# Last chunk's columns in token order, two stores for each PSUM set, and the last evictions shared by two engines

## The chip, the cores and the metric

The kernel runs on one core of a Trainium2 chip. The metric is the device time of one execution in microseconds, and the number used is the median over several executions. PE is the matrix engine (TensorE), DVE is VectorE, ACT is ScalarE, POOL is GpSimd and SP is SyncE, which here issues most DMAs. PSUM is the memory that PE writes its sums to; SBUF is the working memory of the other engines.

## What is computed

Strided sparse attention on 8 batches, 8 heads, 576 positions and 64 columns a head, and after it a dense layer with a rational activation on the 4608 tokens:

```python
scores = scale * np.matmul(q, k.transpose(0, 1, 3, 2))
mask_local = (rel >= 0) & (rel < 32)                        # heads 0..3
mask_strided = (rel >= 0) & (pos[None, :] % 32 == pos[:, None] % 32)   # heads 4..7
attn = softmax(where(mask, scores, -1e9))
x = (attn @ v) as [4608, 512]                               # tokens by (head, column)
h = x @ w_in                                                # 512 -> 2048
P = a[0] + a[1] * h + a[2] * h**2 + a[3] * h**3
Q = 1.0 + abs(b[0]) * abs(h) + abs(b[1]) * h**2
out = (P / (Q + 1e-6)) @ w_out                              # 2048 -> 512, float32
```

## The kernel before

**Chunks.** The dense layer works on nine chunks of 512 tokens. Chunks 0 to 7 are the first 512 positions of each batch. Chunk 8 (NCH - 1) holds the last 64 positions of all eight batches; its inputs are gathered in XW by one transpose for each batch, while chunks 0 to 7 take theirs from XT.

**One chunk.** `dense1(c)` multiplies by w_in: for each pair of the 16 blocks of hidden columns PE fills one PSUM set of two banks (128 x 2 x 512), and ACT copies it to HB as bf16 (L972, the "eviction"). In every chunk the columns of HB are tokens in a permuted order: in chunk 8 the order is (batch, g, i), where position 512 + 4 i + g of the batch is meant. DVE then works out numerator and denominator with nine kinds of instruction (L986 to L1037), and ACT takes 1/Q as Exp of minus Ln (L1010, L1013). L1037 multiplies the two and ends the activation. `dense2(c)` multiplies by w_out: two PSUM sets for each chunk, i2 = 0 and 1, each with two blocks of 128 tokens. A set is evicted to one of two f32 buffers OS (L1103 on ACT, and for the last set of chunk 8 L1100 on DVE) and goes out with four stores of 128 KB (L1060), one for each block (e_) and each half of the partitions (z). SP issues them.

**The last chunk.** Chunk 8 is also the tail of the kernel (`tail`). Its two sets lie in PSUM "A" and "S" (set A and set S here) and are filled in turn, in steps of two blocks of hidden columns, as L1037 delivers them. Its activation is done in groups of 8, 4, 2 and 2 blocks; of the other late chunks each is one group of 16.

**Attention.** One step of the main loop takes one batch: loads of q, k and v by POOL, scores on PE, Exp on ACT, the product with v on PE, normalisation on DVE (L878, L880) into XR, and a DMA transpose of XR into XT or XW (L910, issued by SP). The transposes of q and k into sT (L673) and of the rest of q and k into LT (L684) are SP's, too; a small copy from LT to kL is ACT's (L687), written with a step of 4 elements.

**The order of work.** Every operation is given to `add(engine, instruction, dependencies, cost, key, ...)`. The order in which each engine works is written out by hand in `ORDER`: the n-th operation added has rank ORDER[n], and each engine's queue is sorted by rank. Costs and keys do not enter. Where an operation depends on another engine's, a wait for a semaphore is put in front of it, and an engine's queue is never left out of order: what stands behind a waiting instruction waits, too. On SP this holds for stores and transposes in one queue.

Of the kernel before, what the change touches and what calls it, by code (L numbers as in the profile page):

```python
# [6 lines left out]
AF = mybir.ActivationFunctionType  # L7
# [8 lines left out]
def _bf16_bits(x):  # L16
# [7 lines left out]
    3, 10, 7, 85, 6, 136, 33, 29, 40, 17, 30, 32, 16, 78, 80, 31, 34, 88, 90, 69, 96, 43, 72, 60, 42, 39,  # L24
    74, 45, 103, 112, 64, 110, 105, 91, 101, 92, 62, 1, 14, 5, 21, 8, 28, 4, 24, 13, 12, 15, 11, 2, 9, 52,
    56, 61, 41, 59, 94, 133, 137, 20, 23, 27, 44, 49, 51, 19, 18, 25, 22, 55, 83, 87, 68, 53, 71, 66, 26,
    36, 47, 50, 35, 46, 57, 65, 54, 58, 75, 79, 82, 86, 115, 67, 70, 73, 98, 102, 95, 97, 100, 108, 111, 93,
    99, 106, 114, 117, 77, 107, 116, 129, 128, 132, 135, 139, 183, 37, 81, 76, 84, 104, 126, 130, 109, 122,
    123, 121, 120, 127, 113, 48, 38, 89, 63, 145, 147, 0, 118, 153, 163, 156, 166, 134, 143, 142, 146, 150,
    157, 154, 164, 170, 176, 119, 125, 138, 140, 148, 152, 167, 151, 155, 160, 169, 171, 175, 124, 131, 158,  # L30
    162, 165, 179, 188, 173, 178, 180, 185, 216, 223, 161, 172, 174, 186, 189, 192, 195, 211, 234, 200, 208,
    214, 218, 226, 263, 196, 206, 191, 198, 212, 221, 219, 229, 240, 248, 258, 285, 310, 264, 299, 267, 270,
    282, 290, 301, 318, 181, 184, 187, 190, 193, 182, 194, 204, 209, 224, 228, 231, 233, 244, 255, 236, 239,
    245, 249, 259, 177, 201, 205, 253, 250, 256, 266, 278, 283, 144, 141, 149, 159, 210, 215, 197, 217, 203,
    202, 213, 199, 207, 220, 168, 227, 235, 238, 274, 271, 243, 241, 222, 232, 284, 225, 297, 230, 237, 242,
    246, 252, 257, 260, 262, 265, 269, 261, 276, 279, 308, 320, 293, 298, 300, 302, 303, 306, 309, 313, 312,
    315, 317, 319, 321, 326, 327, 329, 335, 356, 381, 399, 268, 273, 272, 281, 287, 307, 311, 324, 333, 336,
    342, 350, 357, 367, 371, 296, 305, 288, 294, 328, 334, 338, 346, 383, 347, 363, 374, 382, 390, 403, 314,
    322, 304, 316, 331, 340, 325, 332, 353, 378, 385, 418, 441, 406, 427, 392, 398, 429, 447, 457, 459, 254,
    251, 247, 291, 289, 348, 349, 286, 280, 292, 344, 295, 277, 275, 339, 355, 351, 341, 395, 394, 366, 369,  # L40
    364, 361, 362, 358, 323, 330, 337, 343, 365, 370, 376, 380, 386, 393, 387, 405, 408, 417, 415, 411, 419,
    421, 425, 430, 434, 435, 437, 438, 445, 446, 449, 450, 454, 455, 458, 460, 485, 533, 540, 345, 354, 352,
    360, 359, 373, 368, 377, 379, 389, 384, 388, 396, 401, 391, 397, 409, 424, 436, 448, 487, 475, 511, 467,
    476, 500, 529, 568, 581, 453, 481, 488, 503, 512, 535, 557, 592, 400, 413, 422, 433, 439, 523, 532, 442,
    520, 443, 451, 456, 462, 471, 543, 536, 558, 547, 404, 375, 372, 431, 416, 428, 412, 410, 423, 426, 414,
    402, 420, 407, 474, 495, 466, 477, 517, 514, 486, 504, 505, 497, 489, 508, 490, 510, 499, 479, 472, 468,
    463, 465, 461, 452, 432, 440, 464, 469, 483, 491, 494, 498, 506, 470, 509, 515, 525, 526, 542, 546, 548,
    549, 550, 553, 555, 561, 563, 566, 567, 572, 571, 576, 579, 582, 583, 611, 636, 661, 473, 480, 484, 496,
    507, 521, 537, 544, 528, 539, 545, 551, 559, 564, 552, 560, 570, 580, 584, 664, 675, 593, 624, 600, 605,
    639, 685, 651, 700, 603, 612, 617, 637, 658, 674, 689, 719, 478, 493, 502, 518, 556, 671, 627, 693, 668,  # L50
    565, 575, 587, 595, 599, 744, 737, 647, 735, 482, 524, 444, 541, 501, 534, 522, 538, 530, 516, 492, 513,
    531, 519, 586, 597, 594, 596, 620, 623, 589, 616, 609, 606, 608, 590, 602, 610, 625, 622, 630, 604, 527,
    554, 578, 562, 573, 577, 585, 588, 598, 615, 621, 631, 569, 591, 640, 646, 648, 650, 655, 656, 659, 666,
    669, 672, 678, 676, 680, 681, 684, 683, 686, 688, 690, 694, 708, 726, 789, 601, 619, 626, 635, 642, 660,
    654, 662, 663, 670, 677, 682, 687, 692, 667, 679, 697, 704, 710, 756, 792, 769, 784, 728, 733, 803, 819,
    749, 813, 721, 746, 752, 771, 777, 791, 798, 832, 607, 613, 632, 698, 711, 804, 748, 801, 806, 715, 730,
    739, 759, 781, 886, 840, 884, 812, 574, 634, 645, 657, 653, 638, 629, 641, 618, 649, 614, 644, 633, 628,
    709, 699, 706, 702, 741, 731, 723, 718, 727, 720, 716, 701, 712, 724, 738, 732, 729, 773, 652, 643, 665,
    673, 691, 696, 703, 707, 713, 717, 722, 743, 695, 740, 750, 763, 762, 766, 770, 776, 780, 786, 790, 797,
    814, 800, 807, 815, 818, 817, 822, 823, 825, 827, 860, 874, 878, 705, 714, 725, 736, 753, 765, 767, 775,  # L60
    774, 779, 783, 787, 794, 799, 778, 795, 809, 816, 824, 871, 894, 879, 889, 843, 847, 858, 922, 911, 916,
    839, 855, 861, 876, 883, 892, 900, 934, 788, 805, 811, 821, 828, 837, 905, 882, 834, 833, 849, 865, 887,
    899, 910, 931, 936, 907, 764, 734, 772, 768, 757, 758, 745, 754, 760, 742, 755, 761, 747, 751, 848, 830,
    838, 836, 880, 872, 869, 859, 853, 864, 846, 857, 867, 862, 844, 850, 842, 852, 793, 782, 785, 796, 802,
    810, 820, 826, 829, 835, 841, 854, 808, 831, 863, 870, 866, 895, 897, 898, 901, 902, 908, 909, 914, 915,
    918, 919, 921, 923, 925, 926, 928, 929, 946, 961, 963, 845, 851, 856, 868, 873, 877, 875, 885, 881, 888,
    890, 893, 896, 903, 891, 906, 913, 920, 927, 957, 967, 943, 948, 940, 942, 954, 970, 973, 978, 935, 947,
    950, 956, 962, 971, 975, 981, 904, 912, 917, 924, 930, 937, 939, 933, 966, 932, 938, 952, 958, 964, 997,
    996, 990, 993, 941, 945, 949, 953, 955, 960, 944, 951, 965, 969, 972, 976, 979, 983, 959, 980, 984, 991,
    994, 1008, 1025, 1012, 1029, 1000, 1003, 1044, 1048, 1017, 1035, 1001, 1005, 1009, 1018, 1023, 1030,  # L70
    1040, 1053, 968, 974, 977, 982, 986, 1019, 992, 987, 998, 988, 995, 1004, 1007, 1011, 1015, 1013, 1034,
    1016, 985, 989, 999, 1006, 1010, 1021, 1002, 1024, 1038, 1047, 1049, 1064, 1072, 1060, 1078, 1059, 1063,
# [210 lines left out]
def bass_strided_sparse_attn__then__act_rational_pade_kernel(nc, q, k, v, moe_w_in, moe_w_out, moe_a, moe_b, out):  # L283
# [11 lines left out]
    P = 34.0  # L295
# [44 lines left out]
    OS = [A(f"OS{i}", [128, 2, 512], F32) for i in range(NO)]  # L340
# [277 lines left out]
    def ca(n):  # L618
        return 0.19 + n * 0.000833
# [554 lines left out]
```

## Time and profile before

| what | value |
|---|---|
| median of 11 runs | 370.87 us (367.21 to 376.05) |
| profiled execution, its own time | 370.07 us |
| profiled execution, its span | 368.3 us |
| instructions | 9765 |
| PE / DVE / ACT / POOL busy in the span | 86% / 85% / 77% / 41% |
| last matmul ends | 352.3 us |
| last eviction ends | 353.5 us |
| stores | 72 of 128 KB |

The profile is of one execution, with times from the start of its span. The span is 1.8 us shorter than the execution's own time, and that execution ran 0.8 us below the median. Busy shares are averages over stages that differ: up to about 86 us inputs and the first batches set the time, from there to 290 us attention and dense work are mixed, and from 290 us only the dense layer's last two to three chunks are left.

### The profile page before, as it was taken

To read this page: it belongs to the slowest core of one execution; us is meant where nothing else is said; L and a number is where in the kernel's file an instruction comes from. 1 tells how busy PE (TensorE), PEld (TensorE's weight loads), DVE (VectorE), ACT (ScalarE), POOL (GpSimd) and SP (SyncE) were. 2 spreads that over 40 slices of the span, in tenths; PEclk is the share of its full clock that TensorE was granted. 3 is DMA by queue.
4 is the path that set the end of the run, shared out by engine and by line. 5 is a ranking of instruction groups with operands and counts; after the bars stand their busy time and mean duration, and the time that the engine had idled before them with its cause. 6 is when DMAs were issued, how large, how long until landed. Compare 5 with 4: busy or idle time off the path is not lost.

```text
span 368.3 us, 9765 instructions
## 1 busy us (share of the span) xinstructions
PE 316.5 (86%) x4350; PEld 160.4 (44%) x4388; DVE 311.8 (85%) x280; ACT 285.1 (77%) x233; POOL 149.2 (41%) x216
## 2 busy tenths in 40 slices
PE   0669797998999999999699996999999999999920
PEld 0445455444455444544254453444444455554400
DVE  0464999979999997998799899967999899999910
ACT  1324988987998996899789999599899699978510
POOL 1899598308930894498069706600000000000000
PEclk9999999999999999999989999899999999999985
DMA  8999989999978899998989699814501212213212
GB/s 215 214 127 199 204 91 142 139 191 77 126 98 117 89 131 144 147 113 86 167 84 150 65 139 126 111 44 74 102 0 23 59 41 63 67 45 77 51 40 74
DMA packets 95481, 39.12 MB, mean 106 GB/s; under 512 B 66640, under 2 KB 90384, under 8 KB 95440
## 3 DMA queue, kind: packets, MB, share of 16 engines
q0 software_dynamic: 55104, 16.79, 46.4%
q1 hardware_dynamic: 40336, 21.72, 29.8%
q8 instruction: 34, 0.56, 0.7%
q14 instruction: 7, 0.06, 0.1%
HBM read 36.90 MB, written 9.44 MB: 126 GB/s over the span
## 4 chain that ended last, share of the span: by engine, by line
PE 60%; DVE 19%; DMA 10%; SPq 4%; issue 3%; ACT 1%; DVEq 0%
PE psO L613 28%; PE psH L613 18%; PE psS L613 9%; DMA XT<-XR 4%; PE psA L613 4%; DVE XR L880 2%; DVE T L1031 2%; DMA T<-in_v_dram 2%; DVE T L1037 2%; DVE UU L1001 2%; DMA XW<-XR 2%; DMA sT<-qn 2%; DVE T L1029 2%; DVE T L986 1%; DVE UU L998 1%
## 5 line engine op out<-in xcount | busy, mean ns | idle before, releaser
L613 PE MATMUL psO<-Wout,T 128*128 128x512 bf16 x478 | 110.9, 379 | 5.2 <-issue 2.9
L613 PE MATMUL psH<-XT,Win 128*128 128x512 bf16 x336 | 81.8, 385 | 4.0 <-DMA XT<-XR 3.9
L1010 ACT ACTIVATE UU<-UU,cst 128x2048 bf16<-128x2048 bf16 (+1 forms) x38 | 72.2, 1911 | 1.8 <-DVE UU L1001 1.8
L613 PEld LDWEIGHTS psO<-Wout,T 128*128 128x128 bf16 x512 | 48.4, 98 | 57.2 <-issue 1.4
L1013 ACT ACTIVATE UU<-UU 128x2048 bf16<-128x2048 bf16 (+1 forms) x38 | 68.9, 1823 | 0.1
L972 ACT ACTIVATE HB<-psH 128x1024 bf16<-128x1024 f32 x48 | 49.1, 1022 | 15.7 <-PE psH L613 14.7
L613 PEld LDWEIGHTS psH<-XT,Win 128*128 128x128 bf16 x336 | 30.7, 97 | 42.6 <-DMA XT<-XR 4.3
L1037 DVE TENSOR_TENSOR T<-T,UU 128x4096 bf16<-128x4096 bf16 (+2 forms) x23 | 41.9, 1821 | 1.6 <-ACT UU L1013 1.5
L1001 DVE TENSOR_TENSOR UU<-UU,T 128x4096 bf16<-128x4096 bf16 (+2 forms) x23 | 41.9, 1821 | 0.3
L1027 DVE TENSOR_TENSOR T<-T,HB 128x8192 bf16<-128x8192 bf16 (+3 forms) x17 | 41.0, 2414 | 0.2
L1031 DVE TENSOR_TENSOR T<-T,HB 128x8192 bf16<-128x8192 bf16 (+3 forms) x17 | 40.9, 2408 | 0.1
L505 POOL DMA_DIRECT2D VL<-in_v_dram x24 | 19.9, 834 | 47.9 <-PE psA L613 47.4
L998 DVE TENSOR_SCALAR UU<-T,coef 128x4096 bf16<-128x4096 bf16 (+2 forms) x23 | 26.2, 1139 | 0.3
L880 DVE TENSOR_TENSOR XR<-psA,RC 128x512 bf16<-128x512 f32 (+1 forms) x35 | 21.9, 624 | 4.2 <-DMA XT<-XR 1.8
L1020 ACT ACTIVATE T<-HB,coef 128x4096 bf16<-128x4096 bf16 x6 | 22.8, 3796 | 3.1 <-DVE UU L1001 3.1
L526 POOL DMA_DIRECT2D VT<-in_v_dram x32 | 24.4, 782 | 0.2 <-issue 0.2
L1029 DVE TENSOR_SCALAR T<-T,coef 128x8192 bf16<-128x8192 bf16 (+3 forms) x17 | 23.4, 1376 | 0.2
L484 POOL DMA_DIRECT2D tm<-in_q_dram x32 | 20.6, 648 | 6.8 <-DMA HB<-in_q_dram 6.8
L613 PE MATMUL psO<-XT,Win 128*128 128x512 bf16 x96 | 22.7, 378 | 0.7 <-ACT HB L972 0.7
L484 POOL DMA_DIRECT2D tm<-in_k_dram x32 | 21.3, 692 | 4.3 <-DMA LT<-tm 4.3
L1034 DVE TENSOR_SCALAR T<-T,coef 128x8192 bf16<-128x8192 bf16 (+3 forms) x17 | 22.8, 1342 | 0.2
L475 POOL DMA_DIRECT2D kn<-in_k_dram x14 | 15.1, 1082 | 19.1 <-PE psS L613 10.4
(166 smaller groups left out, 460.3 us busy)
## 6 DMA issues: line engine op xcount, KB each, us to landing
out_dram<-OS SPq DMA_DIRECT2D x72, 128.0 KB
kn<-in_k_dram POOLq DMA_DIRECT2D x14, 256.0 KB, 7.4
qn<-in_q_dram POOLq DMA_DIRECT2D x14, 256.0 KB, 7.4
Win<-in_moe_w_in_dram POOLq DMA_DIRECT2D x4, 512.0 KB, 8.3
Wout<-in_moe_w_out_dram POOLq DMA_DIRECT2D x1, 2048.0 KB, 18.9
VL<-in_v_dram POOLq DMA_DIRECT2D x24, 72.0 KB, 3.7
HB<-in_k_dram SPq DMA_DIRECT2D x2, 512.0 KB, 5.9
HB<-in_q_dram SPq DMA_DIRECT2D x2, 512.0 KB, 6.3
```

The source lines that it names most:

```text
L484: add("POOL", (lambda e, h=h, r0=r0: e.dma_start(tm[r0:r0 + 16, :].rearrange("x (g y d) -> x y g d", g=4, y=2)[:, h % 2], src[b, h, 512:57 ...
L613: return lambda e: e.matmul(out_ap, l, r, start=start, stop=stop, skip_group_check=True)
L880: o3 = add("DVE", (lambda d, rc=rc, x=x, src=src, nh_=nh_: d.tensor_tensor(x[:, 0:64 * nh_].rearrange("x (h d) -> x h d", h=nh_), src[:, : ...
L972: o2 = add("ACT", (lambda a, hb=hb, ps=ps, f=f: a.activation(hb[:, f:f + 2, :], ps[:, :, :], AF.Copy)), [o1, old], ca(1024), key.of("HB"))
L998: d2 = add("DVE", (lambda d, u=u, t3=t3, sl=sl, HG=HG: d.tensor_scalar(u[:, 0:HG, :], t3[:, sl, :], b1_ap, b0_ap, op0=Alu.mult, op1=Alu.add)),
L1001: d3 = add("DVE", (lambda d, u=u, t3=t3, sl=sl, HG=HG: d.tensor_tensor(u[:, 0:HG, :], u[:, 0:HG, :], t3[:, sl, :], op=Alu.mult)), [d2], ct ...
L1010: ln = add("ACT", (lambda a, u=u, zl=zl: a.activation(u[:, zl, :], u[:, zl, :], AF.Ln, bias=cst[:, 0:1], scale=1.0)), [d3, cons], 0.28 + w ...
L1013: ex.append(add("ACT", (lambda a, u=u, zl=zl: a.activation(u[:, zl, :], u[:, zl, :], AF.Exp, scale=-1.0)), [ln], 0.21 + w * 0.000833, kz + ...
L1027: d5 = add("DVE", (lambda d, hb=hb, t3=t3, g_=g_: d.tensor_tensor(t3[:, g_, :], t3[:, g_, :], hb[:, g_, :], op=Alu.mult)), [d4], ctt(n), k ...
L1029: d6 = add("DVE", (lambda d, t3=t3, g_=g_: d.tensor_scalar(t3[:, g_, :], t3[:, g_, :], a_ap[1], None, op0=Alu.add)), [d5], cts(n, 1), key ...
L1031: d7 = add("DVE", (lambda d, hb=hb, t3=t3, g_=g_: d.tensor_tensor(t3[:, g_, :], t3[:, g_, :], hb[:, g_, :], op=Alu.mult)), [d6], ctt(n), k ...
L1037: d9 = add("DVE", (lambda d, t3=t3, u=u, sl=sl, HG=HG: d.tensor_tensor(t3[:, sl, :], t3[:, sl, :], u[:, 0:HG, :], op=Alu.mult)), [d8, ex], ...
```

## The change

It has four parts.

1. In chunk 8, ACT's eviction L972 writes HB in token order (batch, i, g). It reads PSUM as before, in the order (batch, g, i), and so writes runs of 16 elements with a step of 4. The DVE work and the matmuls after it use HB's columns as they come, so the rows of set A and set S are in token order too.
2. A set goes out with two stores of 256 KB instead of four of 128 KB, one for each half of the partitions, with both blocks e in it. For chunks 0 to 7 the rows written are the same. For chunk 8 the destination of a store was 4 x 16 x 512 (g, i, column) and is 64 x 2 x 512 (row, e, column) now.
3. Each of the last two sets is evicted by two engines: ACT copies the first block (512 columns) and DVE the second. A store of these sets depends on both.
4. `ORDER` is a new list of 1113 ranks (before 1147: 36 stores fewer, 2 half evictions more), and it places operations on all engines anew.

Read against the order in which the program adds its operations, the new list does this, in outline. At the start, SP's loads of q, k and v for batch 0 are issued in another order (the k of heads 4 to 7 is ninth, not first), POOL's load of the first quarter of w_in stands second in its queue instead of seventeenth, one conversion of v (into VT) stands after the first of the three conversions into VL instead of before them, and two memsets of EW move. In the middle, most queues have neighbours exchanged. Between the transposes of batches 5 to 7 SP has fewer stores: for example, among batch 6's transposes into sT and batch 4's transpose into XW (around 170 us in the profile of before) no store stands any more, where there was one. From M2 of chunk 5 on, PE's order is nearly the old one; M1 of chunk 8 begins with the fourth of its eight sets, and its last set comes last. On ACT the last Exp instructions of chunk 7 stand behind five of the eight evictions of chunk 8.

```diff
 ORDER = [
-    3, 10, 7, 85, 6, 136, 33, 29, 40, 17, 30, 32, 16, 78, 80, 31, 34, 88, 90, 69, 96, 43, 72, 60, 42, 39,
+    4, 10, 15, 17, 7, 88, 2, 35, 36, 32, 50, 69, 159, 37, 100, 0, 63, 83, 82, 48, 54, 22, 85, 55, 64, 96,
...
-    1138, 1144, 1141, 1142, 1145
+    1106, 1110, 1107, 1108, 1109, 1111, 1112
 ]
...
-                o2 = add("ACT", (lambda a, hb=hb, ps=ps, f=f: a.activation(hb[:, f:f + 2, :], ps[:, :, :], AF.Copy)),
+                hd, hs = hb[:, f:f + 2, :], ps[:, :, :]
+                if c == 8:
+                    hd = hd.rearrange("x f (b i g) -> x (f b) g i", b=8, g=4)
+                    hs = hs.rearrange("x f (b g i) -> x (f b) g i", b=8, g=4)
+                o2 = add("ACT", (lambda a, hd=hd, hs=hs: a.activation(hd, hs, AF.Copy)),
                          [o1, old], ca(1024), key.of("HB"))
...
     def store(c, i2, osl, ev, key):
         go = ch_o[osl].group()
-        for e_ in range(2):
-            m = 2 * i2 + e_
-            for z in range(2):
-                src = OS[osl][64 * z:64 * z + 64, e_, :]
-                if c < 8:
-                    dst = out[576 * c:576 * c + 512, :].rearrange("(x g) o -> g x o", g=8)[2 * m + z]
-                else:
-                    r0 = 576 * (2 * m + z) + 512
-                    dst = out[r0:r0 + 64, :].rearrange("(i g) o -> g i o", g=4)
-                add("SP", (lambda e, dst=dst, src=src: e.dma_start(dst, src)), [ev], 0.6, key.of("OW"), go, 0.45)
+        for z in range(2):
+            src = OS[osl][64 * z:64 * z + 64, :, :]
+            if c < 8:
+                dst = out[576 * c:576 * c + 512, :].rearrange("(x f e z) o -> f z x e o", f=2, e=2, z=2)[i2, z]
+            else:
+                dst = out.rearrange("(f e z r) o -> f z r e o", f=2, e=2, z=2)[i2, z, 512:576]
+            add("SP", (lambda e, dst=dst, src=src: e.dma_start(dst, src)), [ev], 0.6, key.of("OW"), go, 0.9)
         os_free[osl] = go.ops
...
-            if tail and i2 == 1:
-                ev = add("DVE", (lambda d, osl=osl, ps=ps: d.tensor_copy(OS[osl][:, :, :], ps[:, :, :])),
-                         [last, os_free[osl]], 1.15, (base + i2 * P / 2).of("OS"))
+            kos = (base + i2 * P / 2).of("OS")
+            if tail:
+                ev = [add("ACT", (lambda a, osl=osl, ps=ps: a.activation(OS[osl][:, 0, :], ps[:, 0, :], AF.Copy)),
+                          [last, os_free[osl]], ca(512), kos),
+                      add("DVE", (lambda d, osl=osl, ps=ps: d.tensor_copy(OS[osl][:, 1, :], ps[:, 1, :])),
+                          [last, os_free[osl]], 0.66, kos)]
             else:
                 ev = add("ACT", (lambda a, osl=osl, ps=ps: a.activation(OS[osl][:, :, :], ps[:, :, :], AF.Copy)),
-                         [last, os_free[osl]], ca(1024), (base + i2 * P / 2).of("OS"))
+                         [last, os_free[osl]], ca(1024), kos)
```

## The prediction, made before the change was run

> **What bounds the kernel now.** I read the page first (shares by engine, the 40 slices, the chain that ended last), then the busy time in chosen stretches, then the SP queue's own instructions at the end, then the instruction groups of ScalarE by shape. From the page:
>
> ```profile
> span 368.3 us, 9765 instructions
> PE 316.5 (86%) x4350; PEld 160.4 (44%) x4388; DVE 311.8 (85%) x280; ACT 285.1 (77%) x233; POOL 149.2 (41%) x216
> ...
> PE   0669797998999999999699996999999999999920
> ...
> PE 60%; DVE 19%; DMA 10%; SPq 4%; issue 3%; ACT 1%; DVEq 0%
> ```
>
> PE carries the middle, and its last slices are empty: the span goes on for 16 us after the last matmul. The stretches show why (us of the stretch, then busy us and count of PE, PEld, DVE, ACT, POOL, then the granted clock, the share of the 16 DMA engines, GB/s):
>
> ```profile
> 86.00:290.00 204.00, 192.47 (x2553) 93.15 (x2583) 187.99 (x135) 181.99 (x145) 95.14 (x131) 0.98 0.80 98
> 290.00:352.00 62.00, 61.68 (x313) 30.83 (x317) 59.93 (x48) 48.16 (x34) 0.00 (x0) 1.00 0.26 60
> ...
> 340.40:343.00 2.60, 2.60 (x14) 1.19 (x13) 2.60 (x5) 1.82 (x3) 0.00 (x0) 1.00 0.87 202
> 352.50:353.50 1.00, 0.00 (x0) 0.00 (x0) 1.00 (x1) 0.00 (x0) 0.00 (x0) 1.00 0.00 0
> 353.50:366.20 12.70, 0.00 (x0) 0.00 (x0) 0.03 (x1) 0.00 (x0) 0.00 (x0) 0.63 0.25 79
> 366.20:367.50 1.30, 0.00 (x0) 0.00 (x0) 0.00 (x0) 0.00 (x0) 0.00 (x0) 0.50 0.09 36
> 367.50:368.30 0.80, 0.00 (x0) 0.00 (x0) 0.00 (x0) 0.00 (x0) 0.00 (x0) 0.50 0.00 0
> ```
>
> Two things are to be seen. From 290 to 352 us PE and DVE are both full (61.7 and 59.9 of 62), ACT is not (48.2). And from 353.5 on only stores run, at a DMA share of 0.25: four engines of sixteen. These are the eight stores of the last chunk, 8 x 128 KB = 1.05 MB in some 13.9 us, 75 GB/s. The stores of chunk 7 (340.4 to 343.0) are as large each, run at a share of 0.87 and move 202 GB/s. The queue tells the same: SP waited for the last stores alone at the end.
>
> ```profile
> SPq L1060 <- ACT OS L1103: 10.8, 1, 10.8
> SPq L1133 <- DMA out_dram<-OS: 5.4, 1, 5.4
> ```
>
> **The tail, step by step (times of the profiled execution).** Removed: the destination whose slowest dimension is 4, which the last chunk's stores have; the new one has 64 rows there, as every other store already has. So I take the new last stores at chunk 7's 202 GB/s. Set A's last matmul ends at 351.42. Its eviction took 1.02 on ScalarE alone (to 352.46); now ScalarE takes one half (0.60, the row of a 128x512 copy from PSUM) beside VectorE's half (about 0.69: half of the 1.225 of VectorE's 128x1024 copy plus a small fixed part, the same as its other 128x512 f32 rows). VectorE's last multiply ended at 350.3, so it is free: ready at 352.13. SP issues 0.05 later, and in the old trace the first byte moved 1.0 after the first issue (352.50 to 353.5): 353.2. Set S's matmuls end at 352.29, its halves at 353.0 instead of 353.54. Four issues at 0.6 each (the unblocked ones of before; the last four took up to 1.67 because their four engines were full) are done by 354.6, before set A's 524 KB have left at 355.8, so the engines never run dry. 1.05 MB / 202 GB/s = 5.2 us: 358.4. From the last byte to the end of the span 0.8: **359.2 instead of 368.3, a gain of 9.1 us**, of which the split evictions are 0.3 and the engines the rest. A store now holds twice the rows of 2 KB; were the issue to double with them (1.2 each), the last would be issued by 357.0 and land by 358.3, so that bound costs nothing. The change adds one wait: each of these stores waits for two engines instead of one. Behind it on SP stand only the other last stores and the final wait, and behind the new half on VectorE only the second set's half, so nobody else is held up.
>
> Here a rule speaks for more. The Trainium skill, "DMA: Bandwidth & Descriptors", section Specifications, puts the HBM limit of one core at about 358 GB/s; by it the 1.05 MB would take 2.9 us and the gain would be 11.4. The row of this kernel's own sixteen-engine stores is 202 GB/s, and I keep it; the rule stays as the low end of the range.
>
> **The strided eviction.** Eight evictions of chunk 8's hidden columns (L972, 1.02 us each, all on ScalarE between 290 and 335) now write runs of 16 with a step of 4 elements. One row of the trace writes so, the copy into kL:
>
> ```profile
> L687 ACT ACTIVATE kL<-LT 128x128 bf16<-128x128 bf16 x8 | 3.9, 486 | 0.0
> ...
> L795 ACT ACTIVATE EX<-psS 128x128 bf16<-128x128 f32 x6 | 1.7, 284 | 0.0
> ```
>
> The same 128 elements cost 0.20 more than in L795. If that is fixed, eight evictions cost 8 x 0.20 = 1.6 us of ScalarE. If it goes with the elements (1.58 ns each), one takes 2.6 us and the eight cost 12.9. A gain is excluded: nothing is taken off the instruction. The Trainium skill, "Advanced Engine Details and Errata", section SBUF Cachelines, says that a line of 16 bytes gives full speed from two hits on, and a step of 8 bytes has two: by the rule the cost is zero. L687 already denies zero. VectorE's own memsets show no price for separate elements (16 single ones, 68 apart, take 72 ns; 32 contiguous words take 85); so I take the fixed end, 1.6 us, and keep 12.9 for the range. The cover for 1.6 is ScalarE's idle time: 49.5 of the 60 us from 285 to 345 are busy. If that cover is gone (12.9 on 49.5 is over 60), what is late first is the last Exp of chunk 7: five of the eight stand ahead of it in the new order, 5 x 1.58 = 7.9 against some 4.8 of idle ScalarE from 285 to 321, and VectorE's multiply at L1037 (321.05 us) waits for it with 30 us of full VectorE behind. That is 3 to 5 us, not recovered.
>
> **Stores halved in number, and the new order.** SP issues 36 stores instead of 72, so 36 x 0.6 = 21.6 us less on a queue that mostly waits. Where it does not, one store of 1.64 us (169.4) stands in the chain between two transposes, and the new order puts no store there. I take -0.5: at best it returns the 2.8 us that PE was idle from 165 to 182, and it may return nothing, because the transpose behind it took 6.4 whatever stood before it. Twice as large a store in front of a transpose holds its engines for 1.3 us instead of 0.65; three transposes are in the chain after the first store, so at most 2 us are lost.
>
> The rest of the list changes every queue. From 86 us on PE was idle 11.5 us of 204 and then 0.3 of 62, so no order gains more than 11.8; lost is one dip like that from 205 to 230 (3.8 us) for each bad place. At the start POOL's first weight load (512 KB) goes ahead of the small loads while SP's inputs stream: at the page's 215 GB/s that is up to 2.4 us later for the last v rows, and one conversion of 0.62 moves in behind them; two memsets of 0.38 on the chain move away or earlier. VectorE is the chain from 34 to 72 us, so a late start passes on at least that far. I take 0 for the order and -1 to +3.5 for the range.
>
> Sum: -9.1 (tail) + 0.2 (strided, what the cover leaves) - 0.5 (SP) = -9.4. On the profiled execution: 370.07 - 9.4 = 360.7; it ran 0.8 below the median of the runs, so on the median 370.87 - 9.4 = **361.5 us**.
>
> **The rivals.**
> 1. The strided writes are priced by the element: ScalarE gets over-full from 285 on, and 4.5 us of the 9.4 are given back: 366. For it: 1.58 ns an element is the plain reading of L687 against L795. Against it: the memsets, and that the same excess would be a fixed one just as well.
> 2. The new order costs a start of 3 us and one dip of 3.8: 368.3. For it: the start is the part of the lists that changes most. Against it: the bytes before the first attention are the same, and PE's order after 290 is nearly the old one.
> 3. Slower: a store waits at the head of SP's queue for an eviction and holds the transposes behind it. SP waited for evictions up to 12.5 us at a time in the trace. The place is between 200 and 230 us, where stores of chunks 2 and 3 stand ahead of batch 7's transposes. It ends slower only if more than 10.9 us of such a wait reaches PE (9.1 + the 1.8 that count as slower); one full wait gives 370.9 - 9.1 + 12.5 = 374.3. Against it: the old order had more stores in front of the same transposes.
> 4. The last stores still run on four engines: the tail loses only the 0.3 of the split, 370.6. Against it: chunk 7's stores have the new shape of 64 rows already and use all.
>
> **How the numbers follow.** Forecast 0.56 (358 to 364), rival 1 0.27 (364 to 368.5), rival 2 0.10, rival 3 0.05, rival 4 0.02. Half a per cent, 1.85 us, is about what a measurement of this kernel can tell from no change, so faster is below 369.0. Faster: all of the forecast, 0.26 of rival 1, 0.05 of rival 2, together 0.87. Same: 0.01 of rival 1, 0.03 of rival 2 and rival 4, 0.06. Slower: 0.02 of rival 2 (a second dip) and rival 3, 0.07. The range 357.5 to 367.5 holds the forecast with the 358 GB/s end partly in, and most of rival 1; left out are rival 3, rival 4 and the upper parts of rivals 1 and 2, together under 2 in 10.
>
> **What would show it.** Right: the stretch after the last eviction at a DMA share of 0.8 or more and 200 GB/s, some 5 us from first byte to last, and SP's final wait short. The strided step: the mean of L972 on chunk 8, 1.2 us for the forecast, 2.6 for rival 1, with a DVE idle at L1037 released by L1013. The order: PE's last matmul at 351 to 353 us; later than 355 with 1.2 us evictions is rival 2, and a gap of several us at XT or XW transposes near 210 is rival 3. Wrong altogether would be a tail that still lasts over 12 us.

## The result, and the profile after the change

The changed kernel takes 366.32 us (median of 12 executions) against 371.63 us of the kernel before (47 executions beside it). The ratio is 0.9874, with a 95% interval from 0.9846 to 0.9902: 1.26% faster, where the forecast was 2.5%. The measured time lies inside the forecast range, at the 366 us of the first rival. Ratios here leave disturbed executions out, so they can differ a little from the quotient of two medians; one of the twelve here took 656.6 us, with 680 ns for each matmul of its largest group instead of 379, for a cause that no run shows. Each set of runs stands beside its own runs of the kernel before, whose medians lie between 371.5 and 374.4 us.

The profile shown here is of another execution of the changed kernel, of 365.1 us. First four lines of the page, the span, the busy times, PE in 40 slices, and the chain that ended last by engine:

```profile
span 363.2 us, 9743 instructions
PE 317.8 (88%) x4351; PEld 160.8 (44%) x4388; DVE 314.8 (87%) x281; ACT 294.2 (81%) x234; POOL 151.1 (42%) x216
PE   0658697959899999999999999999999999789993
PE 55%; DVE 15%; ACT 10%; DMA 10%; issue 4%; POOL 4%; SPq 1%; DVEq 0%; ACTq 0%
```

The empty slices at the end are gone, as forecast. New are a 7 and an 8 of PE in slices 35 and 36, counted from 1, where the old row had nines, and ScalarE's share of the chain: 10%, where it was 1%. ScalarE's busy time went from 285.1 to 294.2 us. The stretches, with the same columns as before (stretch, busy us and count of PE, PEld, DVE, ACT, POOL, clock, DMA share, GB/s):

```profile
86.00:290.00 204.00, 196.99 (x2761) 96.98 (x2786) 195.60 (x141) 189.61 (x152) 98.96 (x137) 1.00 0.89 107
290.00:356.00 66.00, 61.93 (x311) 30.38 (x316) 60.50 (x48) 57.47 (x33) 0.00 (x0) 1.00 0.18 48
...
358.50:362.00 3.50, 0.00 (x0) 0.00 (x0) 0.00 (x0) 0.00 (x0) 0.00 (x0) 0.83 0.97 260
362.00:363.20 1.20, 0.00 (x0) 0.00 (x0) 0.00 (x0) 0.00 (x0) 0.00 (x0) 0.50 0.12 46
```

The last stores now run at a DMA share of 0.97, 260 GB/s (225 to 244 in a later execution). Before, they ran at 0.25 and 79. The trace's records of single packets agree: up to 16 are in flight at a time, where it was 4 for most of the old tail. But from 290 to 356 us PE is idle for 66.00 - 61.93 = 4.1 us. In the same work before (290 to 352) it was idle for 0.3. SP's waits after 340 us agree with the first point, for the wait for the last stores alone went from 5.4 to 2.8 us:

```profile
SPq L1059 <- ACT OS L1105: 10.2, 1, 10.2
...
SPq L1135 <- DMA out_dram<-OS: 2.8, 1, 2.8
```

What makes PE idle is seen at the eviction that the change edits, L974. One line of it for each PSUM buffer that it reads (count, then shortest, median and longest duration in ns, first and last start):

```profile
L974 ACT ACTIVATE HB<-psH x48: 1005/1024/2559, 33.3 to 339.1; 128x1024 bf16<-128x1024 f32 x48
...
L974 ACT ACTIVATE HB<-psS x12: 1016/1024/2535, 149.4 to 341.3; 128x1024 bf16<-128x1024 f32 x12
```

The median hides the matter: the maximum is 2.5 times the median. In the timeline the eight evictions of chunk 8 take 2.46, 2.56, 2.44, 2.44, 2.44, 2.44, 2.44 and 2.54 us, 19.8 together, where eight plain ones of 1.02 take 8.2. The change costs ScalarE 11.6 us, not the 1.6 of the forecast. (Neighbouring instructions overlap a little in the trace; ScalarE's busy time, which counts overlaps once, rose by 9.1 us.) The waits from 290 to 322 us name who pays (us in total, times, longest):

```profile
PEld psH L611 <- ACT HB L974: 2.8, 2, 1.7
PEld psO L611 <- ACT OS L1105: 2.0, 2, 1.0
PE psH L611 <- ACT HB L974: 1.8, 2, 1.2
PE psO L611 <- ACT OS L1105: 1.5, 2, 0.8
```

Before the change, none of these four stood in that stretch; PE there waited for nobody. Now it waits for ScalarE to empty PSUM, for the slow evictions themselves and for the plain ones (L1105) that are queued behind them. And the chain of waits (start, us, what was at work) runs through ScalarE from 291.7 to 325.5 us, with slow evictions among its links:

```profile
291.74 3.66 ACT HB L974 x2
...
302.79 2.34 ACT HB L974
...
317.35 2.33 ACT HB L974
...
323.06 2.45 ACT HB L974
325.51 0.05 issue
325.56 1.91 PE psH L611 x12
```

The span can be accounted for. From the end of the last eviction to the end of the span it was 368.3 - 353.5 = 14.8 us, and is 363.2 - 357.8 = 5.4: 9.4 less. The last eviction itself takes 0.69 instead of 1.23. Against that, it starts at 357.1 instead of 352.3, 4.8 us later: 3.8 of that is new idle time of PE from 290 us on (4.1 - 0.3), PE's busy time is 1.3 higher in this execution (317.8 against 316.5), and its idle time before 290 us is 0.4 lower, so that 4.7 of the 4.8 are named. Together -9.4 - 0.5 + 4.8 = -5.1 us, which is 363.2 - 368.3.

### The profile page after: what moved, and what is told of

Its sections match the earlier page's. It is cut to its first block, busy times and chain, and to the rows that moved or that the text cites. A ratio compares the mean times of both kernels' runs of the same rounds, so it can differ in the third digit from the quotient of the medians.

```text
span 654.6 us, 9743 instructions
## 1 busy us (share of the span) xinstructions
PE 621.5 (95%) x4351; PEld 234.9 (36%) x4388; DVE 316.4 (48%) x281; ACT 300.7 (46%) x234; POOL 149.4 (23%) x216
## 4 chain that ended last, share of the span: by engine, by line
PE 94%; issue 2%; ACT 2%; DMA 1%; DVE 1%; SPq 1%; DVEq 0%; ACTq 0%
PE psO L611 42%; PE psH L611 27%; PE psS L611 14%; PE psA L611 6%; PE psS L614 2%; DMA MK<-c_mk_v 1%; PE psH L598 1%; ACT OS L1105 0%; ACT kL L621 0%; ACT ES L739 0%; PE psH L614 0%; SPq L548 0%; DVE XR L878 0%; SPq L558 0%; DVE sT L622 0%
## 5 line engine op out<-in xcount | busy, mean ns | idle before, releaser
L611 PE MATMUL psO<-Wout,T 128*128 128x512 bf16 x481 | 234.1, 680 | 8.1 <-issue 7.3
L611 PE MATMUL psH<-XT,Win 128*128 128x512 bf16 x336 | 162.0, 669 | 0.9 <-ACT XT L621 0.7
L611 PEld LDWEIGHTS psO<-Wout,T 128*128 128x128 bf16 x512 | 72.1, 144 | 147.0 <-issue 143.5
L974 ACT ACTIVATE HB<-psH 128x1024 bf16<-128x1024 f32 x48 | 57.6, 1199 | 135.9 <-PE psH L611 135.9
L611 PEld LDWEIGHTS psH<-XT,Win 128*128 128x128 bf16 x336 | 45.6, 142 | 92.0 <-issue 87.3
L1105 ACT ACTIVATE OS<-psO 128x1024 f32<-128x1024 f32 x16 | 16.4, 1023 | 75.2 <-PE psO L611 75.2
L988 DVE TENSOR_SCALAR T<-HB 128x8192 uint16<-128x8192 uint16 (+3 forms) x17 | 21.7, 1283 | 52.7 <-ACT HB L974 52.7
L611 PE MATMUL psO<-XT,Win 128*128 128x512 bf16 x96 | 46.7, 675 | 0.0
L611 PE MATMUL psS<-XT,Win 128*128 128x512 bf16 x80 | 39.2, 674 | 0.0
L473 POOL DMA_DIRECT2D kn<-in_k_dram x14 | 11.6, 830 | 59.9 <-DMA sT<-kn 26.5
L611 PE MATMUL psH<-XW,Win 128*128 128x256 bf16 (+1 forms) x72 | 23.6, 526 | 0.0
L1031 DVE TENSOR_SCALAR T<-T,coef 128x8192 bf16<-128x8192 bf16 (+3 forms) x17 | 23.3, 1369 | 0.2
```

Of the source, the lines that this page charges most:

```text
L611: return lambda e: e.matmul(out_ap, l, r, start=start, stop=stop, skip_group_check=True)
L974: o2 = add("ACT", (lambda a, hd=hd, hs=hs: a.activation(hd, hs, AF.Copy)), [o1, old], ca(1024), key.of("HB"))
L1031: d6 = add("DVE", (lambda d, t3=t3, g_=g_: d.tensor_scalar(t3[:, g_, :], t3[:, g_, :], a_ap[1], None, op0=Alu.add)), [d5], cts(n, 1), key ...
```

## The experiments

My theory after the result: the step in ScalarE's write is priced by the element and gives back some 4 us (theory W). The rivals: the new order of work costs it; or the stores gained less than forecast.

### The step alone: left out, and moved to the other side

The changed kernel again, to stand beside the next two runs on the same chip.

> The changed kernel once more, for a profile at full clock and its time beside the others. Both theories expect about 0.987 of the kernel before (367 us). The theory of the step (chunk 8's evictions at 2.4 to 2.5 us each over-fill ScalarE) expects the last matmul 4 to 5 us later than before (356 to 357), with VectorE idle for 3 us or more at the multiply of chunk 7 by 1/Q, released by ScalarE's Exp, and PE idle after that; before 290 us no more than 1 us of difference. The theory of the order (the new list loses the time) expects the last matmul as late, but the time lost before 290 us, on PE waiting for transposes or loads. Both expect the tail after the last matmul to be 9 us shorter.

It took 365.65 us, ratio 0.9821 (0.9758 to 0.9883). The last matmul ends at 357.0 us, as the theory of the step asked, and PE's idle time before 290 us is that of before within 0.4 us. VectorE's idle time at the multiply was 2.2 us, less than the 3 it asked for. Next, the reorder left out:

```
-                if c == 8:
-                    hd = hd.rearrange("x f (b i g) -> x (f b) g i", b=8, g=4)
-                    hs = hs.rearrange("x f (b g i) -> x (f b) g i", b=8, g=4)
```

> The changed kernel with chunk 8's evictions written contiguously, in the old column order; so the reordering of the last 64 rows of each batch is left out. Everything else, the order list too, is that of the changed kernel. Theory of the step: all that was given back returns, 0.975 to 0.978 of the kernel before, the evictions at 1.02 us and the last matmul at 351 to 353 us. Theory of the order: no difference to the changed kernel, 0.987.

It took 362.2 us, ratio 0.9717 (0.9649 to 0.9785), a little below what the theory of the step expected. Then the same pairs of source and destination, walked in the other order, so that the write is in sequence and the read of PSUM has the step, 16 words of 4 bytes:

```
-                    hd = hd.rearrange("x f (b i g) -> x (f b) g i", b=8, g=4)
-                    hs = hs.rearrange("x f (b g i) -> x (f b) g i", b=8, g=4)
+                    hd = hd.rearrange("x f (b i g) -> x (f b) i g", b=8, g=4)
+                    hs = hs.rearrange("x f (b g i) -> x (f b) i g", b=8, g=4)
```

> The changed kernel with the loops of chunk 8's evictions exchanged: ScalarE reads PSUM with a step of 16 words and writes HB contiguously; the same values land in the same places. If the price lies in the write into SBUF, an eviction takes about 1.02 us and the time is 0.976 of the kernel before; if ScalarE pays for a step on either side, 2.4 us or more and 0.987 or above. The theory of the order expects 0.987 whatever the eviction takes.

It took 361.18 us, ratio 0.9699 (0.9633 to 0.9765), 4.5 us below the changed kernel on that chip. Its lines for the eviction, and the stretch from 290 to 322 us, first of the changed kernel, then of this version:

```profile
L974 ACT ACTIVATE HB<-psH x48: 1002/1023/1070, 32.7 to 331.5; 128x1024 bf16<-128x1024 f32 x48
...
L974 ACT ACTIVATE HB<-psS x12: 1014/1023/1046, 146.3 to 332.4; 128x1024 bf16<-128x1024 f32 x12
```

```profile
290.00:322.00 32.00, 28.55 (x152) 14.73 (x154) 30.70 (x14) 31.29 (x17) 0.00 (x0) 1.00 0.13 33
```

```profile
290.00:322.00 32.00, 31.79 (x167) 16.29 (x169) 31.72 (x16) 28.97 (x19) 0.00 (x0) 1.00 0.15 38
```

No eviction of 2.4 us is left, and PE is full again. So the step in the write is shown to be the cost, and a step in the read of PSUM is free: 1.02 us either way. (The intervals of the changed kernel and of this version still touch; those of a second pair below, which also differs in the step alone, do not.) The version with the step in the read stands as low as the one with no reorder at all.

### The engines of the last stores alone

The kernel before, with its order, its four stores for each set and its evictions; only the last chunk's destination is changed to 64 rows in sequence:

```
-                    dst = out[r0:r0 + 64, :].rearrange("(i g) o -> g i o", g=4)
+                    dst = out[r0:r0 + 64, :]
```

> The kernel before, in which only the last chunk's stores go to 64 consecutive rows instead of 4 x 16; the rows of the last 64 positions of each batch then stay in the old column order (the reordering is left out). Four stores a set, unsplit evictions, the old order. The theory of the tail (four engines of sixteen held the end) expects a DMA share of 0.8 or more after the last eviction, the last byte 5 to 6 us after the first, and 8.5 to 9 us less: 0.976. If the tail were bound by SP's issue of eight stores, it would gain under 4 us: 0.989 or above.

It took 364.18 us beside 372.75 before, ratio 0.9778 (0.9719 to 0.9837): 8.3 us. Its stretches after the last eviction:

```profile
356.70:361.70 5.00, 0.00 (x0) 0.00 (x0) 0.00 (x0) 0.00 (x0) 0.00 (x0) 0.77 0.88 204
361.70:362.80 1.10, 0.00 (x0) 0.00 (x0) 0.00 (x0) 0.00 (x0) 0.00 (x0) 0.50 0.12 28
```

Eight stores of 128 KB on all engines move at 204 GB/s, almost exactly the 202 that the forecast took from the stores of chunk 7, in the 5 us that it named. The tail is the main gain of the change, and it was sized rightly: 8.3 us where 8.5 to 9 were expected.

### Once more on another chip, and the order of work

The version with the step in the read, again:

> The changed kernel with the step of the reorder on the PSUM read, once more, as the neighbour of the next two on one chip. The result is that of the reference. Theory W (what costs is a step in ScalarE's write): ratio to before near 0.970, as in the earlier run of it, eight evictions of 1.02 us each for chunk 8. If the earlier gain was of that chip alone: 0.98 or more.

361.54 us, ratio 0.9681 (0.9619 to 0.9743): as in the first run of it. Beside it the same program in the old order of work (the order list rewritten so that each queue keeps its old relative order):

> The changed kernel with the PSUM-side step, but in the order of work of before: each queue's instructions stand in their old relative order, of each four old stores the first and the third place are used, and the last sets' evictions are split as in the change. Theory W, in which the new order is worth nothing on balance (4 us of matmul work later by 86 us, regained in the dips at 165 to 182 and 205 to 230 us): within 1 us of its neighbour with the new order, ratio near 0.970 +- 0.003. Rival O (the new order costs time: its later start is not regained in full): o_old faster than its neighbour by 2 us or more, 0.964 or less. Rival O' (the new order earns part of the gain): o_old slower by 2 us or more, 0.976 or more.

359.48 us, ratio 0.9603 (0.9544 to 0.9661). On this chip it is lower by 2 to 3 us, which spoke for rival O, though the two intervals overlap. What the new order does is seen at the start. The first 86 us of the version in the new order, and of the one in the old order (from a later run of the same program):

```profile
0.00:86.00 86.00, 57.10 (x1275) 32.92 (x1281) 57.23 (x91) 44.70 (x47) 50.88 (x78) 0.94 1.09 149
```

```profile
0.00:86.00 86.00, 63.87 (x1485) 37.44 (x1488) 61.39 (x98) 53.60 (x56) 55.46 (x84) 0.98 1.16 165
```

The new order has done 1275 matmuls by then, and the old 1485; the new order makes it up later, with fewer idle stretches: from 165 to 230 us PE is busy for 62.3 of 65 us, and in the old order for 57.4. Up to 290 us PE's idle time comes to 35.8 us in the new order and 34.5 in the old, so these two executions leave about 1 us of the late start. How much is left over at the end comes again below.

### The step moved into the matmuls

Here the eviction reads and writes in sequence, and the matmuls of chunk 8 read their moving operand in token order:

```
-    makers.append(mm(ps[:, e_, :], Win[:, kk, w], xw[:, kk - 2, :, 64:128], kk == 2, False))
+    makers.append(mm(ps[:, e_, :], Win[:, kk, w], xw[:, kk - 2, :, 64:128].rearrange(
+        "x b (g i) -> x b i g", g=4), kk == 2, False))
...
-    ps[:, e_, :].rearrange("x (b g s y) -> x s b g y", b=8, g=4, s=2)[:, pi],
-    Win[:, kk, w], xw[:, kk, :, 32 * pi:32 * pi + 32], False, kk == 1))
+    ps[:, e_, :].rearrange("x (b s y g) -> x s b y g", b=8, g=4, s=2)[:, pi],
+    Win[:, kk, w], xw[:, kk, :, 32 * pi:32 * pi + 32].rearrange(
+        "x b (g y) -> x b y g", g=4), False, kk == 1))
```

> The changed kernel with the reorder taken out of the eviction altogether: chunk 8's evictions read and write in sequence, and the token order is made by the matmuls of that chunk, which read their moving operand with a step of 8 or 16 elements. The result is that of the reference. Theory W: evictions 1.02 us; if a stepped moving read is free on TensorE, the time is that of the PSUM-side step, 0.970; if it costs what the stepped write costs ScalarE (about 1.4 ns more for each column), the matmuls of chunk 8 grow and TensorE, which bounds that stretch, ends later by several us: 0.98 or more.

413.79 us, ratio 1.1083 (1.1026 to 1.114). The matmuls by shape, first of this kernel, then of its neighbour with the step in the read (count, busy us, mean ns of one):

```profile
L611 PE MATMUL psH<-XW,Win 128*128 128x256 bf16 x48 | 22.8, 608 | 0.0
L611 PE MATMUL psH<-XW,Win 128*128 128x512 bf16 x24 | 22.6, 1032 | 0.0
```

```profile
L611 PE MATMUL psH<-XW,Win 128*128 128x256 bf16 x48 | 7.2, 273 | 0.0
L611 PE MATMUL psH<-XW,Win 128*128 128x512 bf16 x24 | 7.1, 379 | 0.0
```

The price is again one for each column: (608 - 273) / 256 = 1.31 ns and (1032 - 379) / 512 = 1.28 ns. With the 16 and 8 matmuls into the third buffer it makes 64 x 0.335 + 32 x 0.653 = 42.3 us of PE, on the engine that bounds the stretch. That is most of the 52 us by which it is slower than its neighbour. Beside it, the 148 matmuls into psO from 290 to 390 us take 471 ns in the mean, where the neighbour's take 379: 13.6 us more. The granted clock is 0.76 and 0.80 in the two halves of that stretch, and 1.00 in the neighbour's from 290 to 340 us; that the clock is the cause is not shown. The two together are some 4 us more than the 52, and what offsets these is not shown.

### What makes a step dear

The changed kernel with another pattern in each of chunk 8's eight evictions:

```
+                    wr = {6: 4, 0: 2, 2: 8, 4: 16, 8: 32}
+                    if f in wr:
+                        g_s = wr[f]
+                        hd = hd.rearrange("x f (b i g) -> x (f b) g i", i=16, g=g_s)
+                        hs = hs.rearrange("x f (b g i) -> x (f b) g i", i=16, g=g_s)
+                    elif f == 10:
+                        hd = hd.rearrange("x f (b i g) -> x (f b) i g", b=8, g=4)
+                        hs = hs.rearrange("x f (b g i) -> x (f b) i g", b=8, g=4)
+                    elif f == 12:
+                        hd = hd.rearrange("x f (b g i) -> x (f b) g i", i=16, g=2)
+                        hs = hs.rearrange("x f (b i g) -> x (f b) g i", i=16, g=2)
+                    else:
+                        hd = hd.rearrange("x f (h s t) -> x s (f h) t", s=2, t=2)
+                        hs = hs.rearrange("x f (h s t) -> x s (f h) t", s=2, t=2)
```

> A look at durations only: the changed kernel in which each of chunk 8's eight evictions of 1024 columns has another pattern, so its output is in another order than the reference's. In the order of their places: write with a step of 8 bytes (as in the change), 4 bytes, 16 bytes, 32 bytes, 64 bytes; read of PSUM with a step of 16 columns and write in sequence; read of PSUM with a step of 2 and write in sequence; runs of two columns on both sides. Theory L[...]: 4 and 8 bytes alike, 16 bytes and more dearer. Theory N (any write that does not follow its neighbour costs the same 1.4 ns more): 4 to 64 bytes all near 2.45 us, the two with the step in the read 1.02 us, runs of two columns between (about 1.7 us) or at 1.02 us if two adjacent columns (4 bytes) are the unit of a write. Theory R (any step costs, also in a read of 2): the read with a step of 2 is above 1.5 us.

It took 370.14 us in its one execution. The timeline of the eight (start, us), in the order of the expectation: write steps of 8, 4, 16, 32 and 64 bytes, read steps of 16 and of 2 columns, runs of two columns on both sides:

```profile
291.51 2.46 ACT L986 ACTIVATE HB<-psS 128x1024 bf16<-128x1024 f32 x1 [0.71 <-PE psS L611]
293.71 1.41 ACT L986 ACTIVATE HB<-psH 128x1024 bf16<-128x1024 f32 x1
301.89 4.75 ACT L986 ACTIVATE HB<-psH 128x1024 bf16<-128x1024 f32 x1
311.93 4.49 ACT L986 ACTIVATE HB<-psH 128x1024 bf16<-128x1024 f32 x1
320.82 4.69 ACT L986 ACTIVATE HB<-psH 128x1024 bf16<-128x1024 f32 x1
328.91 1.00 ACT L986 ACTIVATE HB<-psH 128x1024 bf16<-128x1024 f32 x1
344.29 1.01 ACT L986 ACTIVATE HB<-psH 128x1024 bf16<-128x1024 f32 x1
345.19 1.02 ACT L986 ACTIVATE HB<-psS 128x1024 bf16<-128x1024 f32 x1
```

Theories L, N and R are all refuted as I had put them: 4 and 8 bytes are not alike (L), the steps do not all cost the same (N), and a read with a step of 2 is free (R). The time grows 1.7 and 1.9 times with the doublings of the step from 4 to 16 bytes and then stays: 1.41, 2.46, 4.75, 4.49, 4.69. So a line of 16 bytes does matter, but not in the way of the rule that the forecast weighed (the Trainium skill, "Advanced Engine Details and Errata", section SBUF Cachelines: two hits on a line are needed to absorb the latency, from which I read full speed at two). With two single elements to the line this eviction takes 2.46 us, with four still 1.41, and only the writes in sequence and those in runs of two run at 1.02. As an estimate from these five, a visit to a line of single elements costs some 4.4 ns: 256, 512 and 1024 visits and a fixed 0.2 us would be 1.3, 2.5 and 4.7 us. The row that the forecast read fits it, too: L687 writes 128 elements with the step of 8 bytes, 64 visits, which makes 0.48 us, and it took 0.486. Runs of two adjacent columns are outside that formula, at 1.02 us with 256 visits of four elements each. I give it as a description of single elements, and the mechanism behind it stays open. Both stepped reads cost nothing.

### Is the new order made for the slow evictions?

The next runs are from a third chip. The changed kernel again:

> The changed kernel again, as the neighbour of the next three on one chip. Ratio to before 0.982 to 0.988, as twice before.

365.72 us beside 371.53, ratio 0.9863 (0.9811 to 0.9915). And the change as it is, step in the write, but in the old order:

> The change as it is, with the step in ScalarE's write, but in the order of work of before; the result is that of the reference. Additive theory (step of the write 4.4 us, new order about 2.5 us, tail the rest): 2 to 3 us below the changed kernel, and 4 to 5 us above o_old2. Rival: the new order is made for the dear evictions and hides part of them, so that the old order with the step in the write is no faster than the changed kernel (within 1 us, or slower).

367.22 us, ratio 0.9889 (0.9838 to 0.9941). The additive theory missed: this is not 2 to 3 us below the changed kernel but 1 us above it, which the intervals can't tell from equal. And the version with the step in the read, in the old order:

> The kernel with the PSUM-side step and the order of before once more, on this chip. If the new order costs time: 0.960 to 0.965 again, 6 to 8 us below the changed kernel. If the earlier difference of 2.9 us to the new order was of that chip: 0.968 or more.

359.65 us, ratio 0.9688 (0.964 to 0.9736). The two differ in the step alone. By the ratios the step in the write costs 0.9889 - 0.9688, some 7.5 us, in the old order, and the intervals are clear of each other; in the new order, on the first chip, 4.5. Their stretches from 290 to 340 us, first with the step in the write (an execution of 370.6 us), then in the read (357.6 us):

```profile
290.00:340.00 50.00, 45.12 (x233) 22.67 (x236) 42.62 (x24) 45.89 (x26) 0.00 (x0) 1.00 0.21 53
```

```profile
290.00:340.00 50.00, 49.74 (x257) 25.32 (x260) 49.72 (x33) 42.13 (x28) 0.00 (x0) 1.00 0.28 72
```

PE loses 4.6 us there. In the new order it loses 3.8 in the same stretch (28.55 + 17.43 = 45.98 busy, against 31.84 + 17.90 = 49.74 of the second run with the step in the read). So the order takes off at most about 1 us of it where it can be seen; the direction is that of the rival, the size is not settled.

### Two stores instead of four, and the split evictions

The kernel before with the step in the read and the last rows in sequence, nothing else:

```
+                if c == 8:
+                    hd = hd.rearrange("x f (b i g) -> x (f b) i g", b=8, g=4)
+                    hs = hs.rearrange("x f (b g i) -> x (f b) i g", b=8, g=4)
...
-                    dst = out[r0:r0 + 64, :].rearrange("(i g) o -> g i o", g=4)
+                    dst = out[r0:r0 + 64, :]
```

> The kernel of before with two edits alone: chunk 8's evictions put the columns in token order with the step on the PSUM read, and the last chunk's stores name 64 rows in sequence; still four stores for each PSUM set and the last two sets evicted by one engine each. The result is that of the reference. If the two edits are all that earns: 0.975 to 0.979 is the engines alone as measured before, so about that. o_old2 against it is then what two stores instead of four and the split evictions bring together: by the forecast 0.3 us for the split, up to 1.6 us in SP's issue at the end (the eight stores were issued in 4.94 us, the four in 3.02) and 0.5 us in the middle, 2.4 us. If they bring more than 4 us, SP's relief in the middle is larger than forecast.

364.81 us, ratio 0.9832 (0.9788 to 0.9875), so 5.2 us above its neighbour with two stores and the split. That was more than the forecast's sizes allow. So I took the two parts apart in a second round on the same chip, where the kernel before took 373.31 us. Four stores again:

> The kernel of before with the step on the PSUM read and the last chunk's rows in sequence, four stores for each set, once more: ratio 0.978 to 0.983, as the two runs of its kind.

364.12 us, ratio 0.9747 (0.9688 to 0.9806). That is lower than expected: the same program on the same chip stands at 0.9832 in one round and at 0.9747 in the other, 3.2 us apart, though the intervals overlap. Two stores without the split:

```
-            if tail:
-                ev = [add("ACT", (lambda a, ...: a.activation(OS[osl][:, 0, :], ps[:, 0, :], AF.Copy)),
-                      ...
-                      add("DVE", (lambda d, ...: d.tensor_copy(OS[osl][:, 1, :], ps[:, 1, :])),
-                      ...
+            if tail and i2 == 1:
+                ev = add("DVE", (lambda d, ...: d.tensor_copy(OS[osl][:, :, :], ps[:, :, :])),
```

> The same with two stores for each PSUM set, in the order of work of before; the last two sets are evicted by one engine each, as before. Theory S (half as many issues on SP are worth several us): 4 us or more below four_again, and within 1 us of o_old3. Rival F (the forecast's sizes: 0.5 us from SP in the middle, up to 1.6 at the end): 1 to 2 us below four_again. Rival N (the difference was one of executions, not of kernels): within 1 us of four_again.

362.75 us, ratio 0.9736 (0.969 to 0.9782). And two stores with it:

> The same with the split evictions too. By every theory 0.3 to 0.6 us below o_old_nosplit; against four_again as o_old_nosplit, 0.3 to 0.6 more. If it is again 5 us below four_again and o_old_nosplit is not, the split carries it, by something that no reading of the trace has shown.

363.95 us, ratio 0.9713 (0.9648 to 0.9779). By the ratios the two parts together bring 0.34%, 1.3 us, here: rivals F and N can't be told apart, and theory S is refuted in this round. (The split's own share can't be told from nothing: by the ratios it brings 0.9 us, and by the medians it costs 1.2.) From the last matmul to the end of the span it is 354.1 to 361.5 with four stores, 358.6 to 364.9 with two, and 349.7 to 355.8 with two and the split (the earlier run): 7.4, 6.3 and 6.1 us. So the end shows 1.3 us of it, nearly all by the stores. The remaining difference in the earlier round lies before the last matmul, and there single executions differ by about as much: the kernel with the last stores' destination alone changed runs the program of the kernel before up to that point, and came there at 355.4 us against 352.3. Whether the relief of SP earns anything in the middle stays open, between nothing and 4 us.

## Why the prediction was right and where it failed

- **Bound and place of the gain: right.** The old tail ran on four engines, the new one on sixteen. The engines alone brought 8.3 us (forecast 9.1, of which 0.3 for the split). In the profile of the change the tail gave 9.9 us (9.4 after the last eviction, 0.5 in that eviction), more than the 9.1; this fits its stores of 256 KB, which moved at 260 GB/s where 202 were assumed.
- **The strided eviction: this is the step that failed.** The prediction had both ends, 0.2 us for each eviction if the excess of L687 over L795 was fixed, and 2.6 us for each eviction if it went with the elements. It took the fixed end, and the trace of the change shows 2.44 to 2.56, an excess of 1.4 us for each eviction or 1.4 ns for each element. At that price 128 elements cost 0.18 us, so the row's excess of 0.20 us is explained by its elements, with next to nothing fixed (the two rows also differ in source and function). What led away from it was a row of another engine, VectorE's memsets, and a hope that a small number stays small. ScalarE's term was 1.6 us and measured 11.6. In the prediction's sum, where it stood with +0.2 us after the cover, 4.5 us reached the end in the new order, the size that rival 1 had named. (A slip without effect on the result: rival 1's 5 x 1.58 = 7.9 us takes the price in ns of one element for the excess in us of one eviction, which is 1.62, so 8.1.)
- **Who waits: not as rival 1 had it.** Rival 1 let VectorE's multiply wait for the last Exp of chunk 7. That wait is there, 2.2 us before the multiply at 323.2 us. But 3.45 of PE's 4.1 us of idle time lie between 290 and 322 us, nearly all in waits for PSUM that ScalarE has not emptied, and the chain of waits goes from a slow eviction straight to PE's matmuls at 325.5, past the multiply. So that rival 1's 4.5 us came out to the decimal is partly luck: its own working gave 3 to 5 us, by another wait. A slow eviction hurts twice: whoever needs its result is late (VectorE's L988 waited 1.1 us for it), and whoever needs its PSUM buffer too.
- **The cover: right for a part, wrong as a sum.** 11.6 us were added to ScalarE and 4.5 came out at the end, so idle time took in the rest. But ScalarE was not over-full: it was busy for 55.8 of the 60 us from 285 to 345 (49.5 before), and its longest pause there, 2.4 us up to 334.5, came after PE had waited for it. Idle time at another moment does not cover a buffer that is emptied late.
- **Issue on SP: right in its unit.** A store of twice the rows still takes 0.61 us to issue (median of 36), so the bound of 1.2 fell away. Its worth of 0.5 us in the middle could be neither shown nor refuted.
- **The new order: within its range.** The later start is real, and it is made up for later. Beside the old order it cost 2 to 3 us in one comparison, with the step in the read; with the step in the write it gained 1 us that is no more than the noise. Rival 2 asked for 6.8 us and evictions of 1.2 us, and is refuted.
- **Rivals 3 and 4: refuted.** No store at the head of SP's queue reaches PE between 200 and 230 us: PE is busy there for 24.3 of 25 us from 205 on, where it was 21.2 before. And the tail's share of the engines is 0.97.
- **What is left over.** With the step in the read the change brings 11.2 and 11.9 us (ratios 0.9699 and 0.9681), more than the 9.4 of the forecast. The intervals are 2.4 us wide to each side, so no cause is claimed for the difference.

The version to keep is the change with the step on the PSUM read: 0.9699 and 0.9681 of the kernel before, on two chips, where the change itself stands at 0.98 to 0.99. In the old order of work it was lower still on one chip (0.9603), but at 0.9688 and 0.9713 in two rounds on another, so between the two orders I would not choose.

## What to carry to other kernels

When a reorder can be put on either side of a copy, find a row of the trace for each side and multiply by the elements before taking any excess for a fixed cost: the same permutation was free in the read of PSUM, 1.4 us for each thousand elements in ScalarE's write, and 1.3 us for each thousand in the matmul's moving read. A cost that is taken as small because other time covers it needs the size of that cover beside its dear end as well, not beside its cheap end alone. And when a line of the profile gives one median for many instructions, look at the maximum: six slow ones of 48 don't move a median.

## What the runs showed of the hardware that was not expected

ScalarE's write of single two-byte elements with a step of 8 bytes takes 2.4 times the plain write (2.46 us against 1.02 for 128x1024), with 16 bytes or more 4.4 to 4.7 times (4.49 to 4.75 us), while steps of 2 and of 16 words in its PSUM read cost nothing (1.00 and 1.01 us). TensorE's moving read from SBUF with steps of 16 and 32 bytes costs 1.3 ns more for each column, which makes a matmul of 512 columns 2.7 times as long (1032 ns against 379).
